# Heads held even-first so that W_in loads fill 128 partitions, with keys, queries and values in two transfers each (retention and a gated feed-forward, one core)

## The chip, the cores and the metric

The kernel runs on 1 core of one Trainium2 chip. The metric is the device time of one execution in microseconds (us); the time of a kernel is the median of its runs. A lower time is better. All arithmetic is float32; the two weight matrices arrive as float64 and are converted on the chip.

## What is computed

A retention layer, whose state decays by a factor of its own for every head, feeds a feed-forward layer without a residual path:

```python
batch, n_heads, seq, head_dim = (4, 8, 768, 64)
gamma = 1.0 - 2.0 ** (-5.0 - np.arange(H))
for t in range(S):
    state = gamma[None, :, None, None] * state + np.einsum('bhd,bhe->bhde', k[:, :, t], v[:, :, t])
    y[:, :, t] = scale * np.einsum('bhd,bhde->bhe', q[:, :, t], state)
x = y.transpose(0, 2, 1, 3).reshape(B * S, H * D)      # 3072 x 512
h = x @ w_in                                           # 512 x 2048
g = h * erf(softplus(h))
out = g @ w_out                                        # 2048 x 512
```

## The kernel before

**Retention.** The 768 positions of each of the four batches are cut into chunks of 128, so there are 24 chunks, numbered `j`. A chunk's keys and queries lie in a tile `KQ[j]` of 128 positions by key/query by eight heads by 64, its values in `V[j]`. Before they are used, keys and queries are multiplied by powers of the heads' decay (`ret_scale`, called `K_`, L514), then turned by TensorE against an identity (`ret_transpose`, `T`, L524) and copied out by ScalarE (L530), so that head pairs `2u` and `2u + 1` lie one above the other on 128 partitions. Scores (`S_`, L557), mask (`M`, L569), and outputs and state (`O_`, L597 to L618, and `A`, L804 and L806) follow. The results land in `XC`, the transposed activations, four columns `kk` of 128 partitions each. Head `h` lands in column `h % 4`, on the lower or upper 64 partitions by `h // 4`. Chunks 0 to 3 are made first, before any feed-forward work, in an order written out by hand (L1081 to L1122); later chunks are woven into the feed-forward.

**The decays.** `d_k` (128 positions by 8 heads, in memory in the order of the heads) and `d_s` (the decay of a whole chunk) are the first two transfers of ScalarE's queue (L399, L400). VectorE copies `d_k` into `kq_s` (L444), makes reciprocals from it (L441, L442), and then runs `K_(0, 0)` on the keys of chunk 0, `second_scales` (L451 to L442), which needs `d_s`, and `K_(0, 1)`, in that order. From chunk 6 on, keys and queries are loaded in blocks of 32 by 32 (`load_blocks`, L187), to be turned by VectorE, with scales of their own (`kq_b`, `by_b`, loaded at L469 and L473).

**The weights.** W_in and W_out arrive in 16 pieces of 1 MB. `load_piece` loads one, `conversion` makes float32 of it on VectorE and ScalarE (L313 to L331), and `load_pieces_after` starts the piece that takes the freed place. Because a column `kk` of `XC` holds heads `kk` and `kk + 4`, and rows of W_in must lie on the partitions of the heads that they meet, a piece of W_in is loaded in halves: `r = 0` to partitions 0 to 63 and `r = 1` to partitions 64 to 127. A piece of W_out is loaded to 128 partitions.

**The order of transfers.** Nearly all are issued by SyncE (SP), in program order: chunk 0's keys and queries, then chunks 1 to 3 with their values, then W_in pieces 0 to 3 (values of chunk 3 in between), then chunk 4. From there on W pieces are issued as conversions free their places.

**The feed-forward.** Of the 3072 positions the first 512 go through plain matmuls in four groups (`hidden`, L860; `project`, L896), while the weights arrive; one more group (L980) is plain too, and the rest use a seven-product scheme on 2 by 2 blocks (L951, L1034), for which `sum_in` adds weight blocks beforehand (L344). The program order of every engine is fixed by the code; nothing is scheduled by a planner.

Of the kernel before, what the change touches and what calls it, by code (L numbers as in the profile page):

```python
# [19 lines left out]
P = 128  # L20
C = 128
# [115 lines left out]
def kernel(  # L137
# [13 lines left out]
    nc = tc.nc  # L151
    B, H, S, D = q.shape
    d_model, d_ff = w_in.shape
    HP = H // 2
    NC = S // C
    NJ = B * NC
    n_k = d_model // P
# [4 lines left out]
    DH = d_model // 2  # L162
# [14 lines left out]
    KQ, V, KB = {}, {}, {}  # L177

    NB = JPC + 2

    def load_blocks(to, src):


        for s, d in itertools.product(range(2), range(2)):
            part = slice((2 * s + d) * 32, (2 * s + d + 1) * 32)
            for u in range(HP):
                nc.sync.dma_start(  # L187
                    to[part, u * C : (u + 1) * C].rearrange("p (a d) -> p a d", d=32),
                    src[2 * u + s, :, d * 32 : (d + 1) * 32].rearrange("(a p) d -> p a d", p=32),
                )  # L190

    def load(j):
        b, c = divmod(j, NC)
        if j == JPC - 1:

            x = act.tile([P, N], F32, name="e", bufs=1)
            KQ[j] = x[:, : 2 * d_model].rearrange("p (i h d) -> p i h d", i=2, h=H)
            V[j] = x[:, 2 * d_model : 3 * d_model].rearrange("p (h d) -> p h d", h=H)
        else:
            KQ[j] = loads.tile([P, 2, H, D], F32, name="kq")  # L200
            V[j] = loads.tile([P, H, D], F32, name="v")
        now = slice(c * C, (c + 1) * C)
        if j >= NB:
            KB[j] = loads.tile([P, HP * C], F32, name="kb", bufs=2)
            nc.sync.dma_start(KQ[j][:, 0], k[b, :, now, :].rearrange("h p d -> p h d"))
            load_blocks(KQ[j][:, 1].rearrange("p h d -> p (h d)"), q[b, :, now, :])
            load_blocks(KB[j], k[b, :, now, :])
        for i, src in enumerate((k, q) if j < NB else ()):
            nc.sync.dma_start(KQ[j][:, i], src[b, :, now, :].rearrange("h p d -> p h d"))
        if not early:  # L210
            load_values(j)

    def load_values(j):
        b, c = divmod(j, NC)
        nc.sync.dma_start(V[j], v[b, :, c * C : (c + 1) * C, :].rearrange("h p d -> p h d"))

    kq_s = const.tile([P, NC, 2, H], F32, name="kq_s")
    d_k = const.tile([P, H], F32, name="d_k")
    d_s = const.tile([P, 2, HP], F32, name="d_s")
# [36 lines left out]
    def load_piece(n, *parts):  # L256

        which, i = pieces[n]
        w = raws[place[n]]
        if which == "in":  # L260
            rows = (slice(2), slice(2, 4)) if n == 0 else (slice(4),)
            for part, g, r in itertools.product(parts or (None,), rows, range(2)):
                f = slice(2 * P) if part is None else slice(part * P, (part + 1) * P)
                nc.sync.dma_start(
                    w[r * D : (r + 1) * D].rearrange("p (g f) -> p g f", g=n_k)[:, g, f],
                    w_in[r * DH : (r + 1) * DH, i * 2 * P : (i + 1) * 2 * P].rearrange(
                        "(g p) f -> p g f", p=D
                    )[:, g, f],
                )
        else:  # L270
            for d in range(2):
                nc.sync.dma_start(
                    w.rearrange("p (d f c) -> p d f c", d=2, f=2)[:, d],
                    w_out[i * 2 * P : (i + 1) * 2 * P, d * DH : (d + 1) * DH].rearrange(
                        "(f p) c -> p f c", p=P
                    ),
                )

    def load_pieces_after(n):
        for later in range(n + 1, n_p):  # L280
            if place[later] == place[n]:
                load_piece(later)
                break
# [112 lines left out]
    nc.gpsimd.memset(below, -float(BELOW << 23))  # L396
    ident = const.tile([P, P], F32, name="ident")
    make_identity(nc, ident)
    nc.scalar.dma_start(d_k, decay_k)  # L399
    nc.scalar.dma_start(d_s, decay_s[::D].rearrange("(o s) h -> o s h", o=1).to_broadcast([P, 2, HP]))  # L400
    load(0)

    nc.scalar.copy(idle_out, ident[:, :1])

    for j in range(1, JPC):
        load(j)
        load_values(j - 1)
    load_piece(0, 0)
    load_values(JPC - 1)
    load_piece(0, 1)  # L410
    for n in range(1, 4):
        load_piece(n, 0, 1)
    load(JPC)
    load_values(JPC)

# [24 lines left out]
    def query_scale(c):  # L440
        nc.vector.reciprocal(kq_s[:, c, 1], kq_s[:, c, 0])  # L441
        nc.vector.tensor_scalar(kq_s[:, c, 1], kq_s[:, c, 1], unscale, None, op0=ALU.mult)  # L442
# [5 lines left out]
    by = const.tile([P, H], F32, name="by")  # L448

    def second_scales():  # L450
        nc.vector.reciprocal(by.rearrange("p (h s) -> p s h", s=2), d_s)  # L451
        nc.vector.tensor_tensor(kq_s[:, 1, 0], kq_s[:, 0, 0], by, op=ALU.mult)
        query_scale(1)
        for c in range(2, NC):
            nc.gpsimd.tensor_tensor(kq_s[:, c, 0], kq_s[:, c - 1, 0], by, op=ALU.mult)
# [7 lines left out]
    by_b = const.tile([P, 2, HP], F32, name="by_b")  # L463

    def load_block_scales():
        for s, d in itertools.product(range(2), range(2)):
            part = slice((2 * s + d) * 32, (2 * s + d + 1) * 32)
            for u in range(HP):
                nc.sync.dma_start(  # L469
                    kq_b[part, 0, 0, u],  # L470
                    decay_k[:, 2 * u + s : 2 * u + s + 1].rearrange("(a p) h -> p (a h)", p=32),
                )
        nc.sync.dma_start(by_b[:, 1], decay_s)  # L473

    def block_scales():
        nc.vector.reciprocal(by_b[:, 0], by_b[:, 1])
# [441 lines left out]
    def chunk_of(g):  # L918
        return TCH // SCH + (g - G0) // 2
# [160 lines left out]

    K_(0, 0)  # L1081
    second_scales()
    T(0, 0)
    keep_warm(2)
# [66 lines left out]
    for g in range(G0):  # L1151
        for u in range(FG):

            if g and u == (2 if g == 1 else 0):
                waiting.append((gated, g - 1))
            hidden(g, u)
            run(after[g][u][0])
            if (g, u) == (1, 0):
                room = 0.0
            waiting.extend(after[g][u][1])  # L1160
        gate(g)
        if g:
            for tt in range(TT):
                project(g - 1, tt)
                if g == 1 and tt < 2:
                    waiting.append((K_, 5) if tt else (sub_states, 4))
                elif g == 2 and tt == 0:
                    sub_results(4)
                    sub_begin(5, ps_h)
                    load_block_scales()  # L1170
                    waiting.append((sub_states, 5))
                elif g == 2 and tt == 2:
                    waiting.append((sub_sums, 4))
# [12 lines left out]
    j = JPC + 2  # L1186
# [94 lines left out]
    g, m = NG - 1, chunk_of(NG - 1)  # L1281
# [4 lines left out]
    r, t0 = R[m], m * SCH  # L1286
# [5 lines left out]
    for i in range(2):  # L1292
# [4 lines left out]
        else:  # L1297
            last = ps_h.tile([P, TCH], F32, name="hp")[:, :P]
            a, b = PRODUCTS[3]
# [50 lines left out]
```

## Time and profile before

| what | value |
|---|---|
| time, median of 3 runs | 663.3 us (663.06 to 663.4) |
| profiled execution: first to last instruction (span) | 660.9 us |
| what lies around the span, median less span | 2.4 us |
| TensorE (PE) busy | 655.7 us, 99% |
| VectorE (DVE) busy | 508.4 us, 77% |
| ScalarE (ACT) busy | 280.2 us, 42% |
| moved by DMA | 51.88 MB in 159413 packets |
| clock granted to TensorE | 1.000 |

The profile gives no own time for the profiled execution beside its span, so its time is read as the span and the 2.4 us around it. "Busy" is the time in which an engine had an instruction in work; for TensorE the ends are modelled. In the timeline a line gives start and duration in us, engine, line of the kernel, operation, the tile written and the tiles read, and in brackets how long the engine was idle before it and what ended that. "SPq" and "ACTq" are instructions that issue transfers. Of DMA queues, q1 is SP's and q10 is ScalarE's; a queue's line gives packets, MB, and the time its packets took as a share of 16 engines.

### The profile page before, as it was taken

How to read it: one execution, taken by the hardware profiler on the slowest of the kernel's cores; microseconds unless marked ns; L12 is line 12 of the kernel's file. 1: busy time of each engine (PE TensorE's matmuls, PEld its weight loads, DVE VectorE, ACT ScalarE, POOL GpSimd, SP SyncE). 2: the span in 40 equal slices, each digit the busy share in tenths (PEclk: the TensorE clock that was granted, in tenths of full speed). 3: DMA queues.
4: the chain of work that ended last, by engine and by line, in shares of the span. 5: the costliest groups of instructions: out<-in, count | busy, mean ns of one | idle time of the engine just before them, and what ended most of it. 6: DMA issues, size and time to landing. Idle time of an engine off the chain costs nothing.

```text
span 660.9 us, 15247 instructions
## 1 busy us (share of the span) xinstructions
PE 655.7 (99%) x6200; PEld 557.3 (84%) x6200; DVE 508.4 (77%) x1102; ACT 280.2 (42%) x402; POOL 11.7 (2%) x29
## 2 busy tenths in 40 slices
PE   8999999999999999999999999999999999999998
PEld 7744444576999999999999999999999999999997
DVE  5999999969986786788678678677687688476464
ACT  3468363445534334244254253342432542533440
POOL 1000000110100000000000000000000000000000
PEclk9999999999999999999999999999999999999999
DMA  9999844385753321222222322221231210000000
GB/s 188 223 264 231 211 129 107 63 152 90 144 123 61 85 47 32 67 47 46 70 44 47 73 39 46 42 72 37 44 79 36 46 53 1 2 34 0 1 33 32
DMA packets 159413, 51.88 MB, mean 78 GB/s; under 512 B 143216, under 2 KB 149744, under 8 KB 159344
## 3 DMA queue, kind: packets, MB, share of 16 engines
q1 hardware_dynamic: 157776, 46.72, 32.8%
q0 software_dynamic: 1152, 4.19, 3.4%
q8 instruction: 48, 0.79, 0.5%
q14 instruction: 21, 0.17, 0.1%
q10 hardware_dynamic: 416, 0.01, 0.0%
HBM read 40.39 MB, written 6.29 MB: 71 GB/s over the span
## 4 chain that ended last, share of the span: by engine, by line
PE 98%; DMA 1%; DVE 0%; ACT 0%; issue 0%
PE o L1034 37%; PE hp L951 22%; PE r L951 12%; PE hp L860 8%; PE o L896 8%; PE hp L980 2%; PE r L736 2%; PE hp L628 1%; PE o L772 1%; PE r L524 1%; PE r L557 1%; PE o L604 1%; PE r L751 1%; PE hp L751 1%; DMA kq<-in_k_dram 1%; PE r L772 0%
## 5 line engine op out<-in xcount | busy, mean ns | idle before, releaser
L1034 PE MATMUL o<-w_out_sb,h 128*128 128x256 f32 (+1 forms) x640 | 142.7, 380 | 0.0
L951 PE MATMUL hp<-xs,w_in_sb 128*128 128x128 f32 x988 | 138.1, 275 | 0.0
L1034 PEld LDWEIGHTS o<-w_out_sb,h 128*128 128x128 f32 x640 | 119.5, 190 | 16.6
L963 DVE TENSOR_TENSOR h<-h,hp 128x256 f32<-128x256 f32 x190 | 78.0, 418 | 70.5 <-PE hp L951 65.6
L951 PEld LDWEIGHTS hp<-xs,w_in_sb 128*128 128x128 f32 x988 | 128.4, 192 | 3.0
L1034 PE MATMUL o<-w_out_sb,e 128*128 128x256 f32 x480 | 113.5, 379 | 0.0
L1034 PEld LDWEIGHTS o<-w_out_sb,e 128*128 128x128 f32 x480 | 86.8, 190 | 9.4
L817 ACT ACTIVATE e<-h 128x2048 f32<-128x2048 f32 x22 | 42.1, 1912 | 119.6 <-DVE h L963 119.6
L963 DVE TENSOR_TENSOR h<-h,r 128x256 f32<-128x256 f32 x152 | 56.9, 415 | 22.3 <-PE r L951 21.4
L965 ACT COPY h<-hp 128x256 f32<-128x256 f32 x38 | 14.2, 373 | 130.7 <-PE hp L951 122.7
L951 PE MATMUL r<-xs,w_in_sb 128*128 128x128 f32 x456 | 63.3, 275 | 0.0
L951 PEld LDWEIGHTS r<-xs,w_in_sb 128*128 128x128 f32 x456 | 57.0, 192 | 0.0
L860 PE MATMUL hp<-xT,w_in_sb 128*128 128x512 f32 (+2 forms) x144 | 56.5, 548 | 0.0
L849 DVE TENSOR_TENSOR e<-h,e 128x1024 f32<-128x1024 f32 x42 | 49.2, 1213 | 8.0 <-ACT e L830 8.0
L860 PEld LDWEIGHTS hp<-xT,w_in_sb 128*128 128x128 f32 x144 | 25.8, 190 | 27.0 <-issue 24.6
L951 PE MATMUL hp<-xT,w_in_sb 128*128 128x128 f32 x304 | 46.3, 275 | 0.0
L951 PEld LDWEIGHTS hp<-xT,w_in_sb 128*128 128x128 f32 x304 | 41.5, 192 | 1.4 <-issue 0.5
L830 ACT ACTIVATE e<-e 128x2048 f32<-128x2048 f32 (+1 forms) x23 | 42.1, 1836 | 0.2
L967 ACT ACTIVATE h<-hp 128x256 f32<-128x256 f32 x57 | 21.9, 384 | 29.7 <-PE hp L951 28.3
L951 PE MATMUL r<-xT,w_in_sb 128*128 128x128 f32 x228 | 31.7, 275 | 0.0
L830 ACT ACT_TABLE_LOAD x24 | 30.8, 1283 | 0.4
L951 PEld LDWEIGHTS r<-xT,w_in_sb 128*128 128x128 f32 x228 | 28.5, 192 | 0.0
(164 smaller groups left out, 799.0 us busy)
## 6 DMA issues: line engine op xcount, KB each, us to landing
w_out_sb<-in_moe_w_out_dram SPq DMA_DIRECT2D x14, 512.0 KB, 5.2
kq<-in_k_dram SPq DMA_DIRECT2D x23, 256.0 KB, 4.0
v<-in_v_dram SPq DMA_DIRECT2D x23, 256.0 KB, 3.4
out_dram<-r SPq DMA_DIRECT2D x23, 256.0 KB, 2.9
kq<-in_q_dram SPq DMA_DIRECT2D x288, 16.0 KB, 1.9
kb<-in_k_dram SPq DMA_DIRECT2D x288, 16.0 KB, 1.8
w_in_sb<-in_moe_w_in_dram SPq DMA_DIRECT2D x8, 512.0 KB, 10.1
w_out_sb<-w_out_sb POOLq DMA_DIRECT2D x8, 512.0 KB, 5.3
```

The costliest lines, as they stand in the source:

```text
L736: nc.tensor.matmul(pp[r][col * D : (col + 1) * D, u % 2, t], x[own, u, :], QT[j][own, u, t], start=first(r, col), stop=True, skip_group_ch ...
L751: nc.tensor.matmul(other[a][own, u % 2, D:] if crossed else pp[a][own, u % 2, t], V[j][t, 2 * u + r, :], AM[j][t, r, u, :D], start=crossed ...
L817: nc.scalar.activation(E[g], HS[g], AF.Softplus)
L830: nc.scalar.activation(E[g][:, half], E[g][:, half], AF.Erf)
L849: nc.vector.tensor_tensor(E[g][:, half], HS[g][:, half], E[g][:, half], op=ALU.mult)
L860: nc.tensor.matmul(HP_[ft][:, t], w_in_of(ft, kk), XC[0][:, kk, t], start=(kk == 0), stop=(kk == n_k - 1),)
L896: nc.tensor.matmul(O[0][tt].rearrange("p (d c) -> p d c", d=2), E[g][:, u * TCH + tt * P : u * TCH + (tt + 1) * P], w_out_of(ft), start=(f ...
L951: nc.tensor.matmul(to[:, u, :], w_in_sb[:, s, w, u * P : (u + 1) * P], XS[m](x), start=first and u == 0, stop=True, skip_group_check=True,)
L963: nc.vector.tensor_tensor(h, h, of, op=ALU.add if plus else ALU.subtract)
L965: nc.scalar.copy(h, of)
L967: nc.scalar.activation(h, of, AF.Copy, scale=-1.0)
L1034: nc.tensor.matmul(O[m][i][:, half, at], G[g][a][:, u * P : (u + 1) * P], w_out_sb[:, s, OUT[b], u, at], start=i not in started, stop=(s = ...
```

## The change

The eight heads are held in the order 0, 2, 4, 6, 1, 3, 5, 7. Slot `i` holds head `i % 4 * 2 + i // 4`. The code of the arithmetic keeps its slots, so slot `i` still lands in column `i % 4` of `XC`, on half `i // 4`. Column `kk` then holds heads `2 kk` and `2 kk + 1`, which are 128 consecutive rows of W_in, and a piece needs no halves. Loads of keys, queries and values become two transfers each, one for the even and one for the odd heads; the decays are loaded in the new order.

```diff
+    def head(i):
+        return i % HP * 2 + i // HP
+
+    def load_heads(to, src):
+        for s in range(2):
+            nc.sync.dma_start(to[:, s * HP : (s + 1) * HP], src[s::2].rearrange("h p d -> p h d"))
...                     # load_blocks
-                    src[2 * u + s, :, d * 32 : (d + 1) * 32].rearrange("(a p) d -> p a d", p=32),
+                    src[head(2 * u + s), :, d * 32 : (d + 1) * 32].rearrange("(a p) d -> p a d", p=32),
...                     # load, j >= NB
-            nc.sync.dma_start(KQ[j][:, 0], k[b, :, now, :].rearrange("h p d -> p h d"))
+            load_heads(KQ[j][:, 0], k[b, :, now, :])
...                     # load, j < NB
-            nc.sync.dma_start(KQ[j][:, i], src[b, :, now, :].rearrange("h p d -> p h d"))
+            load_heads(KQ[j][:, i], src[b, :, now, :])
...                     # load_values
-        nc.sync.dma_start(V[j], v[b, :, c * C : (c + 1) * C, :].rearrange("h p d -> p h d"))
+        load_heads(V[j], v[b, :, c * C : (c + 1) * C, :])
...                     # load_piece
-            for part, g, r in itertools.product(parts or (None,), rows, range(2)):
+            for part, g in itertools.product(parts or (None,), rows):
                 f = slice(2 * P) if part is None else slice(part * P, (part + 1) * P)
                 nc.sync.dma_start(
-                    w[r * D : (r + 1) * D].rearrange("p (g f) -> p g f", g=n_k)[:, g, f],
-                    w_in[r * DH : (r + 1) * DH, i * 2 * P : (i + 1) * 2 * P].rearrange(
-                        "(g p) f -> p g f", p=D
-                    )[:, g, f],
+                    w.rearrange("p (g f) -> p g f", g=n_k)[:, g, f],
+                    w_in[:, i * 2 * P : (i + 1) * 2 * P].rearrange("(g p) f -> p g f", p=P)[:, g, f],
                 )
...
-    nc.scalar.dma_start(d_k, decay_k)
+    for s in range(2):
+        nc.scalar.dma_start(d_k[:, s * HP : (s + 1) * HP], decay_k[:, s::2])
     nc.scalar.dma_start(d_s, decay_s[::D].rearrange("(o s) h -> o s h", o=1).to_broadcast([P, 2, HP]))
...                     # second_scales
-        nc.vector.reciprocal(by.rearrange("p (h s) -> p s h", s=2), d_s)
+        nc.vector.reciprocal(by.rearrange("p (s h) -> p s h", s=2), d_s)
...                     # load_block_scales
-                    decay_k[:, 2 * u + s : 2 * u + s + 1].rearrange("(a p) h -> p (a h)", p=32),
+                    decay_k[:, head(2 * u + s) : head(2 * u + s) + 1].rearrange("(a p) h -> p (a h)", p=32),
                 )
-        nc.sync.dma_start(by_b[:, 1], decay_s)
+        for s, w in itertools.product(range(2), range(2)):
+            nc.sync.dma_start(
+                by_b[s * D : (s + 1) * D, 1, 2 * w : 2 * w + 2], decay_s[w * D : (w + 1) * D, s::2]
+            )
```

## The prediction, made before the changed kernel was run

> **What bounds the kernel now.** I read the page first, then the table of stretches, the chain of waits, and the timeline and DMA view of the first 15 us. The page:
>
> ```profile
> span 660.9 us, 15247 instructions
> ...
> PE 655.7 (99%) x6200; PEld 557.3 (84%) x6200; DVE 508.4 (77%) x1102; ACT 280.2 (42%) x402; POOL 11.7 (2%) x29
> ...
> PE 98%; DMA 1%; DVE 0%; ACT 0%; issue 0%
> ```
>
> TensorE is busy for all but 5.2 us, and the chain is TensorE for 98%. Busy can hide waiting, so I cut the span where TensorE's gaps lie:
>
> ```profile
> 0.00:5.10 5.10, 3.36 (x14) 3.06 (x14) 1.28 (x5) 1.48 (x2) 1.64 (x11) 1.00 0.58 122
> 5.10:14.90 9.80, 9.21 (x99) 8.01 (x99) 7.34 (x17) 3.83 (x8) 1.32 (x4) 1.00 1.34 220
> 14.90:60.00 45.10, 45.10 (x349) 26.57 (x350) 41.79 (x74) 26.57 (x38) 0.00 (x0) 1.00 1.07 232
> 60.00:130.00 70.00, 70.00 (x344) 33.68 (x343) 68.75 (x94) 34.26 (x36) 1.67 (x6) 1.00 0.57 144
> 130.00:590.00 460.00, 460.00 (x4926) 423.40 (x4925) 349.99 (x827) 188.48 (x287) 7.02 (x8) 1.00 0.30 60
> ```
>
> The second column is the length, the third TensorE's busy time, the last two the DMA share and GB/s. From 14.90 to 590 us TensorE has no gap at all. Nor is it waiting inside its instructions: the chain has 32 of L896 in 13.73 us, 0.429 each, and their starts keep that spacing from 54 us to the end of the plain groups. So nothing between 15 and 590 us can be made faster by an earlier transfer, and whatever delays TensorE before 15 us is added to the end whole. What sets that start is here (chain, then VectorE's timeline):
>
> ```profile
> 0.81 3.53 DMA kq<-in_k_dram
> 4.36 0.70 DVE kq L514
> 5.11 1.12 PE r L524 x4
> ```
>
> ```profile
> 2.91 0.17 DVE L444 COPY kq_s<-d_k 128x8 f32<-128x8 f32 x1 [2.91 <-DMA d_k<-decay_k_dram]
> 4.36 0.69 DVE L514 TENSOR_TENSOR kq<-kq,kq_s 128x512 f32<-128x512 f32 x1 [0.84 <-DMA kq<-in_k_dram]
> 4.97 0.20 DVE L451 RECIPROCAL by<-d_s 128x8 f32<-128x8 f32 x1
> 5.76 0.69 DVE L514 TENSOR_TENSOR kq<-kq,kq_s 128x512 f32<-128x512 f32 x1
> 6.97 0.69 DVE L514 TENSOR_TENSOR kq<-kq,kq_s 128x512 f32<-128x512 f32 x1 [0.51 <-DMA kq<-in_k_dram]
> 8.25 0.69 DVE L514 TENSOR_TENSOR kq<-kq,kq_s 128x512 f32<-128x512 f32 x1 [0.59 <-DMA kq<-in_q_dram]
> ```
>
> `d_k` is there at 2.9 us and has 0.84 us to spare. After that the loads are the bound: the keys of chunk 0, the keys of chunk 1 (6.97) and its queries (8.25) are each waited for. `d_s` has nearly nothing to spare (landing at 4.6, read at 4.97).
>
> **W_in on 128 partitions.** What it may bring shows in the page's DMA part:
>
> ```profile
> w_out_sb<-in_moe_w_out_dram SPq DMA_DIRECT2D x14, 512.0 KB, 5.2
> ...
> w_in_sb<-in_moe_w_in_dram SPq DMA_DIRECT2D x8, 512.0 KB, 10.1
> ```
>
> Equal sizes, half the partitions, twice the time to landing (the second in a fuller queue). So the pieces should land earlier, and SP issues half as many. But in the whole trace VectorE waits for W_in once, 0.35 us at 19.37 (L313), and TensorE works without a gap through that time. What is late next is the conversion itself (VectorE is busy 68.75 of 70 us from 60 to 130). Gain: 0; if that cover were gone, at most the 0.35 us.
>
> The Trainium skill ("DMA: Bandwidth & Descriptors", Rules for kernel authors) says that two transfers to disjoint partition halves only serialize and advises one over 128. Priced by the rows of landing, the saving in the DMA queues would be about 4.9 us for each 512 KB, and by the trace none of it reaches TensorE.
>
> **Arithmetic.** Instructions, shapes and order of PE, DVE, ACT and POOL stay, slots being renamed. 0.
>
> **Keys, queries, values in halves.** Packets stay 256 bytes and as many. Each extra transfer costs SP one issue; small ones issued back to back stand 0.47 us apart (16 at L469 in 8.74 us). Two halves are 0.95 us of issue against the 1.20 us that a 256 KB load takes at the 218 GB/s of 5 to 13 us, so the DMA engines stay the bound: 0. If SP took 0.65 us each, as at L264, it would be 0.1 us a load, 0.5 us by the keys of chunk 2: upper bound. Later on, six more issues precede the last block of chunk 7's keys (three for `by_b`, one each for keys and values of chunk 6 and keys of chunk 7, less a wait or two that they fill): up to 2.8 us. VectorE waits there already (3.2 us, L546), but afterwards idles 2.26 us before L635 at 147.89, which covers it to within 0.6 us, and TensorE has its own work there. 0.
>
> **`d_k` as two strided halves.** This is where I see a cost. A row of `d_k` is 8 consecutive numbers; every second of them is not consecutive. How the trace moves single numbers from a strided column is seen in `kq_b` (128 numbers a transfer), and how the two queues mix when `d_s` runs beside the loads:
>
> ```profile
> q1 hardware_dynamic: 1309, 0.01, 16.1%
> ...
> kq_b<-decay_k_dram SPq DMA_DIRECT2D x10, 0.5 KB, 1.8
> ```
>
> ```profile
> DMA packets 623, 0.09 MB, mean 134 GB/s; under 512 B 623, under 2 KB 623, under 8 KB 623
> ...
> q1 hardware_dynamic: 366, 0.09, 57.6%
> q10 hardware_dynamic: 257, 0.00, 19.8%
> ```
>
> The first is 92.7 to 97 us: 1309 packets for about ten transfers, one a number, each occupying an engine for 0.161 x 4.3 x 16 / 1309 = 8.5 ns. So `d_k` goes from 128 packets to 1024, and with the end packet per engine of one more transfer ScalarE's queue from 416 to 1328: 912 more, ahead of or among the first keys and queries. Cheapest, they fill engine time alone: 912 x 8.5 / 16 = 0.5 us. But the second view (3.3 to 4.0 us) shows the queues mixed: 623 packets in 0.7 us, 890 a us, against 616 in 0.6 us, 1027 a us, from 2.6 to 3.2 when SP's ran alone. From 3.5 to 4.0 it is 344 in 0.5 us, 690 a us; from 1.8 to 2.6, at the very start, 335 in 0.8 us, 420 a us. So 912 packets cost 1.0, 1.3 or 2.2 us. I take 1.2, between the first two, since they are under load as the new ones will be, and keep 0.5 and 2.2.
>
> All loads behind them land 1.2 us later: chunk 1's keys at 8.1 instead of 6.94. `d_k`'s second half, issued 0.47 us later (ScalarE's two issues stand so), lands about 4.5 to 5.5, eats its 0.84 us and holds `K_(0, 0)` until 5.1 to 6.1; `d_s` behind it lands at about 5.5 to 6.5, and all of VectorE queued behind L451 waits: `K_(0, 1)`, then chunk 1's scaling, and TensorE's transposes behind those. This comes to the same 1 us or so, beside the loads and not on top.
>
> **A slow TensorE at the start.** L495 starts every 213 ns until 6.87 us, the L524 after it every 109, though the granted clock reads 1.00 throughout. With gaps around `T(0, 0)` longer by 1 to 2 us the step may come later than its work. Least: it moves with the chain, 0. Most: some 2.8 us, if all that runs from 7 to 10.5 us is slow (12 transposes at 0.104 and 16 others at about 0.1). I take the four transposes of one group, 4 x 0.104 = 0.4, being nearest to what stands beside the step.
>
> The Trainium skill ("TensorE: Matmul & The Clock Gate", Part 1) explains such a step by a free-running window of about 3.4 us that must be busy. By it, the step would come either with the chain or one window later, and the sum would be 1.2 or about 3.
>
> **Sum.** 0 + 0 + 0 + 1.2 + 0.4 = 1.6 us. Span 660.9 + 1.6 = 662.5; with 2.4 us around it, 664.9 against 663.3 now. A measurement of this kernel can tell about 0.2%, 1.3 us.
>
> **Rivals.**
> 1. The small packets slip into the gaps at 8.5 ns: `d_k` lands inside its spare 0.84 us, loads move 0.5 us at most. Not slower to a measurement: 663.3 to 664.0. For it: the packets are short. Against: both queues slow while mixed, seen twice. It decides if `d_k` lands before 3.75. Chance 0.20.
> 2. `d_s` decides: 1328 small packets, one for each of SP's, at 420 a us: 2656 / 420 = 6.3 us from 1.85, so `d_s` lands at 8.7, `K_(0, 1)` starts at 9.5 for 5.76: +3.7, less what the loads had already lost, and a slow clock with it: 666 to 667.5. For it: the rate at the very start. Against: the later, higher rates. Chance 0.18.
> 3. W_in was after all what TensorE followed, in the conversions: 663.0 at best by the 0.35 us. The span has no other wait for it. Chance 0.03.
> 4. The later SP queue passes its 2.26 us cover: +0.6, 663.9 without the start's cost. Chance 0.05.
>
> **How the numbers follow.** My case (0.9 to 2.3 us later, 664.2 to 665.6) has 0.54; about a quarter of it is within 1.3 us. Same: rivals 1, 3 and 4 and that part, 0.41, of which I give 0.01 away. Slower: the rest of my case and rival 2, 0.58. Faster by 1.3 us has no place to come from but an error of mine: 0.02. The range leaves out the lower half of rival 1 and the far end of rival 2: 663.6 to 667.0.
>
> **What would show it.** In the profile after: q10 with about 1328 packets; L444 waiting for `d_k` until 4.5 to 5.5; first L514 at 5.1 to 6.1; chunk 1's keys at about 8.1; TensorE without gaps from about 16.5 on; W_in landing in near 5 us for 512 KB and TensorE no earlier for it. I am wrong if L444 starts before 3.8, or if a gap in TensorE opens or closes after 17 us.

## The result and the profile after

| kernel | median of 5 runs | lowest to highest | ratio to before |
|---|---|---|---|
| before | 663.4 us | 663.06 to 664.04 | 1 |
| changed | 666.7 us | 665.13 to 668.27 | 1.0051 (1.0037 to 1.0066) |

The changed kernel is slower by 3.3 us. The profiled execution took 665.13 us, the lowest of the five, with a span of 663.4: 1.73 us lie around it. That span is 2.5 us longer than before's 660.9. The page:

```profile
span 663.4 us, 15333 instructions
...
PE 655.3 (99%) x6200; PEld 556.5 (84%) x6200; DVE 508.1 (77%) x1102; ACT 280.1 (42%) x402; POOL 12.1 (2%) x29
...
q10 hardware_dynamic: 1328, 0.01, 0.1%
...
PE 98%; DVE 1%; DMA 0%; ACT 0%; issue 0%; ACTq 0%; DVEq 0%
...
w_in_sb<-in_moe_w_in_dram SPq DMA_DIRECT2D x4, 1024.0 KB, 5.4
```

TensorE does the same 655 us of work, so the 2.5 us are new idle time. ScalarE's queue carries the 1328 packets. Lines of code have moved by about 10: L406 loads `d_k`, L451 copies it, L524 is `ret_scale`, L534 the transposes, L505 the idle products, L556 the scaling of prepared chunks, L961 the products of the seven-product scheme, L973 its additions, L359 GpSimd's transfers. A whole MB of W_in now lands in 5.4 us, where half of one took 10.1. The stretches show where the idle time is:

```profile
0.00:5.10 5.10, 3.35 (x14) 3.06 (x14) 0.23 (x2) 1.47 (x2) 1.63 (x11) 1.00 0.60 98
5.10:15.50 10.40, 8.57 (x102) 7.17 (x102) 8.29 (x20) 3.85 (x8) 1.81 (x4) 1.00 1.28 225
15.50:60.00 44.50, 44.50 (x348) 26.31 (x349) 41.14 (x74) 25.97 (x38) 0.00 (x0) 1.00 0.88 258
60.00:130.00 70.00, 70.00 (x343) 33.41 (x342) 68.83 (x93) 34.34 (x34) 1.68 (x6) 1.00 0.46 127
130.00:590.00 460.00, 458.99 (x4896) 422.29 (x4895) 349.24 (x827) 188.88 (x288) 7.00 (x8) 1.00 0.30 60
```

From 15.5 to 130 us TensorE is full again, but between 130 and 590 it is short by 1.01 us. That gap was not there before. The losses lie in three places.

**The start, 0.57 us.** VectorE's timeline:

```profile
4.83 0.17 DVE L451 COPY kq_s<-d_k 128x8 f32<-128x8 f32 x1 [4.83 <-DMA d_k<-decay_k_dram]
...
5.36 0.69 DVE L524 TENSOR_TENSOR kq<-kq,kq_s 128x512 f32<-128x512 f32 x1
...
6.71 1.51 DVE L524 TENSOR_TENSOR kq<-kq,kq_s 128x512 f32<-128x512 f32 x2
8.85 0.69 DVE L524 TENSOR_TENSOR kq<-kq,kq_s 128x512 f32<-128x512 f32 x1 [0.63 <-DMA kq<-in_q_dram]
```

`d_k` is waited for until 4.83 us (2.91 before), `K_(0, 0)` starts at 5.36 instead of 4.36, and the last of these scalings, on chunk 1's queries, at 8.85 instead of 8.25. The loads themselves came 0.57 us later: chunk 1's keys landed at 7.51, before at 6.94. Not all of this need be the strided `d_k`'s: with the same halves and `d_k` whole they landed at 7.07 in e2 below, though at 6.75 in e5. TensorE's last wait of the start ended at 15.46, before at 14.89.

**A gap at 163 us, 1.28 us.** Timelines of VectorE and GpSimd, first before, then after, and TensorE's after:

```profile
139.30 0.69 DVE L546 TENSOR_TENSOR kb<-kb,kq_b 128x512 f32<-128x512 f32 x1 [3.18 <-DMA kq<-in_k_dram]
```

```profile
137.82 0.87 POOL L353 DMA_DIRECT2D w_out_sb<-w_out_sb  x1 [5.64 <-PE hp L980]
```

```profile
144.37 0.69 DVE L556 TENSOR_TENSOR kb<-kb,kq_b 128x512 f32<-128x512 f32 x1 [7.65 <-DMA v<-in_v_dram]
```

```profile
138.49 0.87 POOL L359 DMA_DIRECT2D w_out_sb<-w_out_sb  x1 [5.75 <-PE hp L990]
```

```profile
163.72 1.16 PE L961 MATMUL hp<-xs,w_in_sb 128*128 128x128 f32 x8 [1.01 <-DVE h L973]
```

SP's issues of chunk 7's blocks (tile view of `kb`, 128 to 146 us; after the count come the durations in ns, then the first and the last start), before and after, and the time to landing after:

```profile
L187 SPq DMA_DIRECT2D kb<-in_k_dram x13: 430/430/1206, 128.0 to 134.8; - x13
```

```profile
L195 SPq DMA_DIRECT2D kb<-in_k_dram x16: 376/430/1297, 130.0 to 139.0; - x16
...
DMA to landing us min/median/max: 1.7/2.3/5.2
```

VectorE waits 7.65 us for chunk 7's block loads, before 3.2. The label names the values, but what VectorE reads is the blocks, of which the last landed at 144.15. SP issued that last block at 138.99 us, before at 134.78 (landing at 138.92). GpSimd's transfer, 512 KB from SBUF to SBUF with an addition, was issued at 138.49, so that it now stands ahead of the block: the block landed after it, 5.2 us after its issue. VectorE is then 5 us behind, and at 162.7 TensorE has to wait for it.

**The end, 0.65 us.** The chain's last instruction of an engine, and SP's waits from 655 us on; first before, then after:

```profile
658.11 0.29 DVE r L1305
```

```profile
SPq L1346 <- DMA out_dram<-r: 0.7, 1, 0.7
```

```profile
659.96 0.29 DVE r L1315
```

```profile
SPq L1356 <- DMA out_dram<-r: 1.0, 2, 0.8
```

From the end of VectorE's last addition to the end of the span it was 660.9 - 658.40 = 2.50 us, and is 663.4 - 660.25 = 3.15. The work after that addition, one store, is the same. SP closes with a row of waits in a fixed order of semaphores, and the 43 additional transfers have turned the last store to another semaphore. Before, one more wait followed the one for it; now five more waits follow, of 0.07 to 0.36 us each.

Those three make 0.57 + 1.28 + 0.65 = 2.5. The 1.28 is the gap of 1.01 and 0.27 more: VectorE's last addition starts 1.85 us later, of which the start and the gap's visible part explain 1.58. This 0.27 for each gap recurs below; what it is, no run shows.

### The profile page after: what moved, and what is told of

It reads as the page before. It is cut to its first block, busy times and chain, and to the rows that moved or that the text cites. A ratio compares the mean times of both kernels' runs of the same rounds, so it can differ in the third digit from the quotient of the medians.

```text
span 663.4 us, 15333 instructions
## 1 busy us (share of the span) xinstructions
PE 655.3 (99%) x6200; PEld 556.5 (84%) x6200; DVE 508.1 (77%) x1102; ACT 280.1 (42%) x402; POOL 12.1 (2%) x29
## 3 DMA queue, kind: packets, MB, share of 16 engines
q10 hardware_dynamic: 1328, 0.01, 0.1%
## 4 chain that ended last, share of the span: by engine, by line
PE 98%; DVE 1%; DMA 0%; ACT 0%; issue 0%; ACTq 0%; DVEq 0%
PE o L1044 37%; PE hp L961 22%; PE r L961 12%; PE hp L870 8%; PE o L906 8%; PE hp L990 2%; PE r L746 2%; PE hp L638 1%; PE o L782 1%; PE r L567 1%; PE o L614 1%; PE r L761 1%; PE hp L761 1%; PE r L534 1%; DMA d_k<-decay_k_dram 0%; PE r L782 0%
## 5 line engine op out<-in xcount | busy, mean ns | idle before, releaser
L961 PE MATMUL hp<-xs,w_in_sb 128*128 128x128 f32 x988 | 138.2, 275 | 1.0 <-DVE h L973 1.0
L961 PEld LDWEIGHTS hp<-xs,w_in_sb 128*128 128x128 f32 x988 | 128.4, 192 | 4.1 <-DVE h L973 1.2
L973 DVE TENSOR_TENSOR h<-h,hp 128x256 f32<-128x256 f32 x190 | 78.0, 419 | 68.1 <-PE hp L961 63.3
L973 DVE TENSOR_TENSOR h<-h,r 128x256 f32<-128x256 f32 x152 | 57.0, 417 | 21.4 <-PE r L961 20.6
L961 PE MATMUL r<-xs,w_in_sb 128*128 128x128 f32 x456 | 63.3, 275 | 0.0
L961 PEld LDWEIGHTS r<-xs,w_in_sb 128*128 128x128 f32 x456 | 57.0, 192 | 0.0
L961 PE MATMUL hp<-xT,w_in_sb 128*128 128x128 f32 x304 | 46.3, 275 | 0.0
L961 PEld LDWEIGHTS hp<-xT,w_in_sb 128*128 128x128 f32 x304 | 41.5, 192 | 1.4 <-issue 0.5
L961 PE MATMUL r<-xT,w_in_sb 128*128 128x128 f32 x228 | 31.7, 275 | 0.0
L961 PEld LDWEIGHTS r<-xT,w_in_sb 128*128 128x128 f32 x228 | 28.5, 192 | 0.0
```

The source lines that it names most:

```text
L961: nc.tensor.matmul(to[:, u, :], w_in_sb[:, s, w, u * P : (u + 1) * P], XS[m](x), start=first and u == 0, stop=True, skip_group_check=True,)
L973: nc.vector.tensor_tensor(h, h, of, op=ALU.add if plus else ALU.subtract)
```

## The experiments

My theory: three costs that add up, namely the strided `d_k` at the start (with TensorE's slow phase), SP's later issues in front of GpSimd's transfer, and the order of the closing waits. Rivals: one of the first two makes it all; the halves as such cost; W_in gains something that the rest hides. Each run's profile is split in the same way in the table. "Start" is by how much later than in before (14.89) TensorE's last wait of the start ended. "Gaps" are TensorE's waits between 19 and 590 us. "Last addition" is by how much later than 658.11 VectorE's last instruction starts. "Tail" is from that instruction's end to the end of the span.

| kernel | start | gaps | last addition | tail | profiled execution | median (lowest to highest, runs) |
|---|---|---|---|---|---|---|
| changed | 0.57 | 1.01 | 1.85 | 3.15 | 665.13 | 666.7 (665.13 to 668.27, 5) |
| e1 changed again | 1.76 | 0.68, 1.57 | 4.55 | 3.15 | 667.83 | 668.06 (666.64 to 668.38, 5) |
| e2 `d_k` whole | 0.20 | 0.99 | 1.45 | 3.25 | 664.8 | 665.36 (664.6 to 666.29, 5) |
| e3 scales early | 1.36 | none | 1.36 | 3.24 | 664.67 | 664.9 (664.67 to 665.56, 5) |
| e4 GpSimd later | 2.11 | 1.60 | 3.98 | 3.12 | 667.27 | 667.0 (663.66 to 672.41, 8) |
| e5 both e2 and e3 | -0.12 | none | -0.11 | 3.21 | 663.25 | 663.55 (663.25 to 665.58, 11) |
| e6 before, strided | 3.02 | none | 3.03 | 2.47 | 666.01 | 666.01 (665.66 to 666.83, 5) |
| e7 before, 3 issues | 1.89 | none | 1.89 | 2.81 | 664.97 | 663.1 (662.94 to 664.97, 11) |
| e8 halves where needed | 1.84 | none | 1.84 | 2.56 | 664.52 | 663.76 (662.61 to 664.52, 11) |
| e9 changed, more warm | 0.64 | 0.89, 1.92 | 3.98 | 3.12 | 667.29 | 667.02 (664.78 to 668.96, 6) |
| e10 before, halves | 0.32 | none | 0.32 | 2.68 | 663.12 | 663.14 (662.78 to 664.71, 12) |
| e11 e8, one more warm | 0.29 | none | 0.29 | 2.51 | 662.96 | 662.94 (662.69 to 663.03, 11) |
| e12 before, less warm | 1.33 | none | 1.33 | 2.47 | 663.95 | 663.72 (663.22 to 665.48, 11) |

Before beside them was 662.91 (e1 to e4), 663.03 (e5 to e8) and 662.96 us (e9 to e12). In each row the last addition's delay is the start's plus the gaps plus 0.26 to 0.27 for each gap, to 0.01 us. So nothing else delayed the last addition. Start and gaps are those of one execution, which need not be like the median's. "Measured" below is the time as a multiple of before's beside it, with its 95% interval. The two groups of runs e1 to e4 and e5 to e12 were taken on different chips.

### e1: the changed kernel once more

> The changed kernel as it is, run and profiled again, to see which of its costs return. Theory A (two costs): TensorE's stream is 0.5 to 0.7 us later by 16 us, for the decays' small packets, and there is a second gap of 1 us or more near 163 us, where VectorE waited 7.7 us for the last blocks of chunk 7's keys because SP issues them some 4 us later and they fall behind a GpSimd transfer. Time 665 to 668 us. Theory B (start alone): the gap near 163 was an accident of one execution and is not there again; what is above 0.6 us is scatter. Theory C (weights): the earlier landing of W_in moves other transfers; gaps would appear between 17 and 130 us.

Measured 1.0073 (1.0061 to 1.0085). VectorE's and TensorE's timelines:

```profile
145.23 0.69 DVE L556 TENSOR_TENSOR kb<-kb,kq_b 128x512 f32<-128x512 f32 x1 [7.33 <-DMA v<-in_v_dram]
...
213.12 0.69 DVE L556 TENSOR_TENSOR kb<-kb,kq_b 128x512 f32<-128x512 f32 x1 [4.88 <-DMA v<-in_v_dram]
```

```profile
164.58 1.16 PE L961 MATMUL hp<-xs,w_in_sb 128*128 128x128 f32 x8 [0.68 <-DVE h L973]
...
218.25 1.16 PE L961 MATMUL hp<-xs,w_in_sb 128*128 128x128 f32 x8 [1.57 <-DVE h L973]
```

The gap is there again, and a second one, where chunk 10's blocks are late (the expectation of e10 calls it chunk 9): their last issue was at 202.0 us before, at 207.9 in the changed kernel's first profile, at 209.4 here. The start differs too, though it waits equally long for `d_k`. TensorE's timeline, the first profile and then e1:

```profile
6.11 0.66 PE L534 MATMUL r<-ident,kq 128*128 128x128 f32 x4 [1.29 <-DVE kq L524]
6.60 0.61 PE L505 MATMUL o<-ident 128*128 128x128 f32 x4
```

```profile
6.11 1.11 PE L534 MATMUL r<-ident,kq 128*128 128x128 f32 x4 [1.29 <-DVE kq L524]
7.01 1.06 PE L505 MATMUL o<-ident 128*128 128x128 f32 x4
```

The same groups after the same wait take 0.66 or 1.11 us. TensorE begins in a slow phase (starts 213 ns apart, later 109), and the traces hold records of the granted clock that tell when it ends: the step to the full clock is at 7.02 us in before, at 5.48 in the first profile after, while TensorE waits, and at 9.91 in e1. Ahead of its first record a trace has none, and the clock column of the stretches reads 1.00 there: the 1.00 "throughout" of the prediction is no measurement. The late step costs e1 1.2 us more at the start.

The records also show what chance this is. From the step to the clock's drop after the kernel's end it is a whole number of 3.413 us in all thirteen traces that have records (192 times in before and in e1, 193 times in the first profile after). So the clock changes on a grid of 3.4 us, and where the grid lies against the kernel's start differs from execution to execution.

### e2 and e3: one of the two suspects each

In e2 `d_k` is loaded whole, and the copy that VectorE makes anyway puts it in order:

```diff
-    for s in range(2):
-        nc.scalar.dma_start(d_k[:, s * HP : (s + 1) * HP], decay_k[:, s::2])
+    nc.scalar.dma_start(d_k, decay_k)
...
-    nc.vector.tensor_copy(kq_s[:, 0, 0], d_k)
+    nc.vector.tensor_copy(
+        kq_s[:, 0, 0].rearrange("p (s h) -> p s h", s=2), d_k.rearrange("p (h s) -> p s h", s=2)
+    )
```

> The changed kernel with one contiguous transfer of d_k, put into the new order by the copy on VectorE that is there anyway. Theory A: L451 starts at about 3 us again, the first L524 at 4.0 to 4.5, TensorE's stream 0.4 to 0.7 us earlier than in the changed kernel; the gap near 163 stays, so 0.5 us less than the changed kernel and still 1 us or more above the kernel before. Theory B: all of the loss goes, 663.4. If the halved loads delay the start themselves, it stays late by more than 0.3 us.

Measured 1.0038 (1.0025 to 1.0051). VectorE's and TensorE's timelines:

```profile
2.72 0.17 DVE L450 COPY kq_s<-d_k 128x8 f32<-128x8 f32 x1 [2.72 <-DMA d_k<-decay_k_dram]
...
4.79 0.69 DVE L525 TENSOR_TENSOR kq<-kq,kq_s 128x512 f32<-128x512 f32 x1 [1.46 <-DMA kq<-in_k_dram]
```

```profile
163.32 1.16 PE L962 MATMUL hp<-xs,w_in_sb 128*128 128x128 f32 x8 [0.99 <-DVE h L974]
```

The copy waits until 2.7 us, the start is back to +0.20, and the gap stays (0.99). What is left at the start goes with the halves: `K_(0, 0)` waits for the second half of chunk 0's keys until 4.79, where it began at 4.36 before.

In e3 the block scales, with the three more issues of `by_b`, are loaded a projection earlier, where SP isn't backlogged:

```diff
                 project(g - 1, tt)
+                if (g, tt) == (1, 3):
+                    load_block_scales()
...
                     sub_begin(5, ps_h)
-                    load_block_scales()
```

> The changed kernel with the 20 transfers of the block scales issued one group earlier, where SP has nothing to do, so that nothing of them stands ahead of chunks 6 and 7. Theory A: chunk 7's last block is issued 1.5 to 3 us earlier and lands ahead of GpSimd's transfer, at about 139 us; VectorE waits 2 to 4 us for it instead of 7.7, no gap near 163; 1 us or more (by the median 2 us) less than the changed kernel, and 0.6 us above the kernel before. Theory B: no change against the changed kernel.

Measured 1.0031 (1.0019 to 1.0043). VectorE's timeline:

```profile
140.29 0.69 DVE L556 TENSOR_TENSOR kb<-kb,kq_b 128x512 f32<-128x512 f32 x1 [2.77 <-DMA kb<-in_k_dram]
...
209.14 0.69 DVE L556 TENSOR_TENSOR kb<-kb,kq_b 128x512 f32<-128x512 f32 x1 [2.25 <-DMA kb<-in_k_dram]
```

The first wait is as short as in before (3.2), the second is 2.25 (before had none there), and both gaps are gone. GpSimd's transfer was issued at 138.98, and the last block, issued at 137.28, landed ahead of it at 140.07. The start keeps its cost. Neither suspect alone makes the loss.

### e4: GpSimd's transfer moved

```diff
-        if n in (1, 4, 7):
+        if n in (1, 7, 8):
             next(last_steps)
```

> The changed kernel with the second and third of GpSimd's accumulating transfers (the sums of W_out) begun after the seventh and eighth step of the plain group instead of after the fourth and seventh, about 7 us later. SP's queue is as in the changed kernel. Theory A: chunk 7's last block, issued at about 139 us, lands at 140 to 141 instead of 144.2; VectorE's wait shrinks from 7.7 to about 4 us; the gap near 163 is gone, 1 us or more less than the changed kernel. If SP's later issue alone were enough without the collision, the gap would stay.

Measured 1.0062 (1.0035 to 1.009), with runs from 663.66 to 672.41. VectorE's and TensorE's timelines:

```profile
143.17 0.69 DVE L556 TENSOR_TENSOR kb<-kb,kq_b 128x512 f32<-128x512 f32 x1 [4.90 <-DMA kb<-in_k_dram]
...
212.55 0.69 DVE L556 TENSOR_TENSOR kb<-kb,kq_b 128x512 f32<-128x512 f32 x1 [4.91 <-DMA kb<-in_k_dram]
```

```profile
217.69 1.16 PE L961 MATMUL hp<-xs,w_in_sb 128*128 128x128 f32 x8 [1.60 <-DVE h L973]
```

The transfer now starts at 144.91, the first wait falls from 7.3 to 4.9 us and its gap is gone, so GpSimd's transfer had its part in the first gap. It has none in the second one, which stays. The median didn't fall against e1 by more than the runs scatter. The run of 672.41 has no profile, but its granted clock is 0.994 on average, where most runs have 0.999 or 1.000: by estimate 0.006 x 670.7 = 4.0 us of it are lost clock.

### e5: both taken away

> The changed kernel with both: d_k in one contiguous transfer, and the block scales issued one group earlier. If the two costs add (start 0.2 instead of 0.6 to 2.1 us late, no gap near 163 or 216), the span is 662.0 and the time 663.6 to 663.9, about 4 us less than the changed kernel measured beside it. What stays above the kernel before is then 0.2 at the start and the longer end: the last store's landing to the end of the span took 1.6 us instead of 0.9 in all profiles of changed kernels. If one of them was only a part of the other, the time stays at 664.5 or more.

Measured 1.0016 (1.0007 to 1.0025). Start -0.12, no gap, and yet a span of 661.5, 0.6 more than before: all of it the tail (3.21). The medians put a price on each cost: the tail, and what else is left, 663.55 - 663.03 = 0.5 us; the strided `d_k` with its slow phase, e3 less e5, 1.35; the late blocks, e2 less e5, 1.8. Together 3.7 us, between the 3.3 and 5.1 (e1) that the changed kernel itself measured. These prices are rough: e2 and e3 have five runs each and ran on another chip than e5, and four of e5's eleven runs are at 664.6 to 665.6.

The second gap goes with something else, which the traces show, though no run tried it. In e1 the last of chunk 10's blocks was still on its way when the queue named `instruction` (q8) began a packet of 16 KB at 210.64 us, which held one of the 16 engines for 1.2 us (73.2% of 16 engines for 0.1 us). First that packet (DMA view of 210.6 to 210.7 us), then the landing of the block issued at 209.44, and for comparison that of the block issued at 207.91 in the first profile after:

```profile
q8 instruction: 1, 0.02, 73.2%
```

```profile
kb<-in_k_dram SPq DMA_DIRECT2D x1, 16.0 KB, 3.5
```

```profile
kb<-in_k_dram SPq DMA_DIRECT2D x1, 16.0 KB, 1.7
```

It is the same in e4 and e9 (packet at 210.01 and 209.73, last block landing at 212.33 and 212.34). In the other eleven profiles the last block had landed when this packet began (in the first profile after at 209.62, before 210.45), and none of them has a second gap.

### e6 and e7: parts of the change, put into before

e6 loads `d_k` in two strided halves, left in the old order:

```diff
-    nc.scalar.dma_start(d_k, decay_k)
+    for s in range(2):
+        nc.scalar.dma_start(d_k[:, s::2], decay_k[:, s::2])
```

> The kernel before with d_k alone loaded as two strided halves (even and odd heads, each to its old place); all else as before. Theory A: L444 starts at 4.6 to 4.9 us, TensorE's stream by 16 us is 0.6 to 2.1 us late, depending on when TensorE's starts at the beginning go from 213 to 109 ns apart; no gap near 163 or 216, end unchanged: 663.5 to 665.0. If the halved loads were needed for the damage, less than 0.3 us late.

Measured 1.0051 (1.0039 to 1.0064). The chain, and the stretches around the delayed start:

```profile
1.49 4.73 DMA d_k<-decay_k_dram
```

```profile
4.70:8.00 3.30, 0.50 (x5) 0.42 (x5) 1.55 (x7) 0.00 (x0) 0.00 (x1) 1.00 1.39 197
8.02:11.43 3.41, 3.41 (x18) 3.03 (x18) 2.57 (x7) 1.24 (x3) 1.90 (x4) 0.50 1.35 218
11.50:14.90 3.40, 3.17 (x41) 2.74 (x41) 1.89 (x3) 1.04 (x2) 0.00 (x0) 1.00 1.35 218
```

That is above the 663.5 to 665.0 expected, and the start loses more than in the changed kernel itself. Here the numbers are strided in SBUF as well, and among whole loads of SP's rather than halves; `d_k` was there only at 6.2 us instead of 4.8. Which of the two differences does it is open. TensorE was idle for 2.80 us, until 7.58, and the granted clock (the column after POOL), which had stepped up at 4.60, is back at 0.50 for one stretch of 3.41 us, from 8.02 to 11.43. TensorE's starts are 213 ns apart again in this stretch: the slow phase is the clock's.

The Trainium skill ("TensorE: Matmul & The Clock Gate", Part 1) says that this clock follows a free-running window of about 3.4 us, so that the same kernel is slow for a different time in each run. The traces agree: steps of 3.413 us, and 5.48 and 9.91 us for the end of the slow phase in the two profiles of the changed kernel. With one such window more the prediction's sum was, by its estimate, about 3 us, 1.8 above the 1.2 without; e1's later step cost 1.2.

e7 has three more transfers than before, by loading chunk 4's keys, queries and values in halves.

> The kernel before with the keys, queries and values of chunk 4 alone in two transfers each (heads 0 to 3 and 4 to 7): three more transfers on SP at about 30 us, where nothing waits, so that the last store signals on another of SP's rotating semaphores, the same as in the changed kernel. If the longer end comes from the place of that semaphore in SP's closing row of waits: TensorE as before throughout, 0.6 to 0.7 us more between the last store's landing and the end, 663.5 to 663.6. If the end has another cause, no change against the kernel before.

Measured 1.0006 (0.9997 to 1.0014): three issues there cost nothing. The profiled execution was the slowest of the eleven, by a late step of the clock (10.98 us), though nothing at its start differs from before. Its tail is 2.81. Six waits follow the one for the last store, of 0.06 us each, where before has one, so the place in the row is worth 0.3 us, which the median doesn't show. The rest of the changed kernel's 0.65 lies in waits that take longer there (one of them 0.36), and why they do is open.

### e8 and e11: the change without its costs

e8 has halves only for the keys and queries of chunks 0 to 5. Values and later keys are loaded whole and read by head; `d_k` is whole, the scales are early, and one transfer of W_in less is split, so that SP makes as many transfers as before, 717.

```diff
-            load_heads(KQ[j][:, 0], k[b, :, now, :])
+            nc.sync.dma_start(KQ[j][:, 0], k[b, :, now, :].rearrange("h p d -> p h d"))
...
-        load_heads(V[j], v[b, :, c * C : (c + 1) * C, :])
+        nc.sync.dma_start(V[j], v[b, :, c * C : (c + 1) * C, :].rearrange("h p d -> p h d"))
...                     # products with values, the same at every use
-                place(h), V[j][:, h, :], AM[j][:, h % 2, h // 2, :],
+                place(h), V[j][:, head(h), :], AM[j][:, h % 2, h // 2, :],
```

> W_in on 128 partitions, with halves only for keys and queries of chunks 0 to 5 (where TensorE's transposes need neighbours); values, and keys from chunk 6 on, in one transfer in the heads' own order, addressed by head; d_k whole, block scales one group earlier, and as many SP transfers modulo 8 as in the kernel before (a second half of W_in's first piece in one transfer). Start 0 to 0.3 us late, no gap, end as before: 662.9 to 663.2, no slower than the kernel before by more than 0.3 us. If 128 partitions for W_in are worth anything by themselves, it shows here as less than 662.9.

Measured 1.0008 (0.9999 to 1.0017), in two groups, five runs from 662.61 to 663.1 and six from 663.76 to 664.52. The median misses the 662.9 to 663.2 expected. The profiled execution is of the upper group, with the step of the clock at 10.87 us. The tail is 2.56, so it does go back with the number of transfers. e11 adds one idle product:

```diff
-    keep_warm(7)
+    keep_warm(8)
```

> The kernel with halves only where needed, d_k whole, block scales early and the number of SP transfers as before modulo 8, with eight instead of seven idle products, which fill the 0.66 us that TensorE waited for chunk 0's keys. Theory A: the slower executions (663.8 to 664.5) go, the time is 662.6 to 663.0, no slower than the kernel before; W_in on 128 partitions gains nothing beyond that. If W_in's faster transfers were worth time, below 662.4.

Measured 0.9997 (0.9989 to 1.0006), all eleven runs within 0.34 us. TensorE's timeline:

```profile
1.46 3.69 PE L510 MATMUL o<-ident 128*128 128x128 f32 x16 [1.46 <-POOL ident masks.py:199]
5.76 0.66 PE L539 MATMUL r<-ident,kq 128*128 128x128 f32 x4 [0.60 <-DVE kq L529]
6.25 0.61 PE L510 MATMUL o<-ident 128*128 128x128 f32 x4
```

The transposes at 5.76 are fast already, and the upper group is gone. With W_in on 128 partitions and none of the other costs, the time is before's, so W_in gains nothing that shows. (Before with eight idle products was not run, so this run alone doesn't tell what the eighth saves from what W_in might; but before's TensorE has no gap from 14.9 to 590 us that W_in could close.)

### e9, e10, e12: the slow phase and the halves by themselves

e9 is the changed kernel with ten idle products at the start for seven.

> The changed kernel with ten instead of seven idle products at the start (L505), so that TensorE is busy until about 6.1 us, when its first transposes can start, instead of idle from 4.8. Nothing that waits for loads changes. Theory A, with the clock: the step from 213 to 109 ns comes by about 7 us in every execution, so the start is 0.6 us late and no longer up to 2.1; the time falls by 0.5 to 1.5 us by the median, and the later gaps (163, 216) stay: 665.5 to 667. If the late step has nothing to do with TensorE's idle time, the time stays at that of the changed kernel, 666.7 to 668.

Measured 1.0055 (1.0038 to 1.0072). The start fell to +0.64, but this execution has both gaps (0.89 and 1.92), and the median is no better than the changed kernel's first one, where 0.5 to 1.5 us less was expected. A better start alone saves nothing that can be told, while the gaps stay.

e10 is before with all loads of keys, queries and values in halves, by the old order (the blocks excepted).

> The kernel before with all loads of keys, queries and values (but for the blocks) in two transfers, heads 0 to 3 and 4 to 7, and nothing else. SP then has three more issues ahead of chunk 7's last block and seven ahead of chunk 9's. Theory A (SP's backlog): the last block of chunk 7 is issued 1 to 2 us later and VectorE's wait there grows from 3.2 to 4 to 8 us, by whether GpSimd's second transfer is met; chunk 9's blocks are 3 to 5 us later; a gap of up to 1.6 us near 163 or 216 in part of the executions; start as before but for the clock: 663.5 to 666. If only by_b's extra issues push SP over, no gap and 663.0 to 663.7.

Measured 1.0006 (0.9997 to 1.0014). VectorE's timeline:

```profile
139.07 0.69 DVE L551 TENSOR_TENSOR kb<-kb,kq_b 128x512 f32<-128x512 f32 x1 [2.65 <-DMA kb<-in_k_dram]
```

The halves alone cost nothing late: the last block is issued at 135.88, and VectorE waits 2.65 us. By the rows it takes `by_b`'s issues as well to push SP past the cover. These are the views of `by_b`, before and after:

```profile
L473 SPq DMA_DIRECT2D by_b<-decay_s_dram x1: 430/430/430, 97.2 to 97.2; - x1
```

```profile
L481 SPq DMA_DIRECT2D by_b<-decay_s_dram x4: 590/601/692, 97.7 to 99.7; - x4
```

One transfer of 0.43 us has become four that hold SP for 2.62 us, 2.2 more. (e3 moved them together with the other block scales, so that they were not tried by themselves.)

At the start the halves don't show in the median, but they aren't free. In this profile the start is 0.32 late, and chunk 0's keys are complete at 4.74 us, before at 4.34. Of the 34 runs of e5, e8 and e10, which load the first chunks in halves and `d_k` whole, 13 are 1.1 us or more above the fastest run of their kernel. Of the 80 runs with before's start (before beside e1 to e12, and e7) three are. With one idle product more (e11) none of eleven is. That it is the clock's late step in all of these is seen in the profiles of e7 and e8 alone.

e12 is before with five idle products for seven; nothing else changes.

> The kernel before with five instead of seven idle products at the start: TensorE is idle from about 4.0 instead of 4.8 us until its first transposes at 5.1; no transfer and no other instruction changes. Theory A, with the clock: in part of the executions the step from 213 to 109 ns comes at 9 to 11 us instead of 6.7 and the time is up to 1.9 us longer; the median 663.0 to 664.9, with a wider spread than the kernel before beside it. If idle time before the step does not matter, 663.0 and no wider.

Measured 1.0013 (1.0004 to 1.0021). TensorE's timeline:

```profile
1.46 2.50 PE L495 MATMUL o<-ident 128*128 128x128 f32 x10 [1.46 <-POOL ident masks.py:199]
5.11 1.12 PE L524 MATMUL r<-ident,kq 128*128 128x128 f32 x4 [1.15 <-DVE kq L514]
6.02 1.06 PE L495 MATMUL o<-ident 128*128 128x128 f32 x4
7.07 1.12 PE L524 MATMUL hp<-ident,kq 128*128 128x128 f32 x4
```

`T(0, 0)` starts at 5.11 as in before, but after 1.15 us of idle time instead of 0.29, and what follows stays slow until the clock's step at 9.91 us, before at 7.02. That alone costs 0.8 us in the median and up to 2.5. So a wait in front of the first transposes costs twice: for itself, and by the phase that it prolongs in part of the executions.

## Why the prediction was right, and where it was not

The direction was right and the time (666.7) lies in the range, but the middle was 1.8 us too low, and that the range held is in part luck. It reached up to 667.0 for rival 2, which didn't come: `d_s` landed at 5.83, not at 8.7 (its own sum, 1.85 + 6.3, gives 8.15). What filled the upper part was a term put at 0, and the same kernel's median in e1, 668.06, lies above the range. Rival 1 didn't come either: `d_k` landed at 4.74, not before 3.75. Step by step:

**W_in, 0 us: right.** The pieces land early, VectorE's 0.35 us wait is gone, and neither the changed kernel nor e11 is earlier for it.

**The halves of the first chunks, 0 us: right for the median (e10), too low for single runs.** Chunk 0's keys are complete up to 0.4 us later (e2, e10), which the upper bound of 0.5 covers, and slow runs, by e8's profile those of a late clock step, come more often.

**`d_k` as 912 more packets, 1.2 us: the mechanism right, the size too large.** The packets are there, L451 waited until 4.83 (named: 4.5 to 5.5) and `K_(0, 0)` started at 5.36 (named: 5.1 to 6.1). But the loads came 0.57 us later, not 1.2: chunk 1's keys at 7.51 and not 8.1, and of this the halves may have a part (7.07 in e2, 6.75 in e5). From 2.3 to 4.2 us the mixed queues moved 2530 packets in 1.9 us, 1330 a us, where I had taken 690 to 890. So the mixed rates in the trace of before were no limit of the engines, presumably those of queues with too little to move, and the row that I kept as the low end, 0.5, was the nearest.

**The slow phase, 0.4 us: a matter of chance, 1.2 us between two profiles of the same kernel.** Both terms together, 1.6 us by the prediction, are 1.35 by e3 less e5.

**Six issues ahead of chunk 7's last block, 0 us: this is the step that failed.** The price of up to 2.8 us of delay and the cover of 2.26 us on VectorE were read from the timeline, and rival 4 gave 0.6 us to the case that it doesn't suffice. But the issue slipped by 4.2 us: 0.57 is the start's, and `by_b`'s three more issues took 2.2, at 0.6 to 0.7 each, where I had priced an issue at 0.47. And I asked only how late it would be and not what starts on the DMA engines meanwhile: GpSimd's 512 KB, at 137.82 in the trace of before, 3 us after that last issue. The block that came behind it took 5.2 us to land, the one just before it 1.8, and the backlog went on to chunk 10. Medians give this 1.8 us, three times rival 4's price. "I am wrong if a gap in TensorE opens after 17 us" was the right alarm; it went off.

**The end, not in the sum: about 0.5 us.** That more transfers can lengthen the closing waits was not on my list. The tails of e5 (3.21, with the change's transfers) and e8 (2.56, with before's number) show it. That it is the last store's place in the row of semaphores is read from the trace and was not tried by itself; e7, with three more transfers, got 0.3 of it.

Open are: how busy TensorE must have been for the clock to step up at a point of its grid (one idle product more made e8's two groups into one), what makes e6 dearer than the same packets in the changed kernel, and most of the scatter of e4.

## What to carry to other kernels

A small table that is reordered by a strided transfer becomes one packet for each number, and whoever reads it first pays; let a copy that an engine makes anyway put it in order. When a change adds transfers to a queue that is backlogged, follow the queue to the next user, and see which other transfers will have started on the DMA engines by then: slack read from a wait is worth nothing if a long transfer stands in it. A wait ahead of TensorE's first work is dearer than it looks, as it can prolong the slow phase (e12); fill it with idle products, and compare medians of many runs, not single profiles.

## What the runs showed that I had not expected

- Two executions of one kernel, with the same waits until 6.11 us, differ by 1.2 us in the next 10 us by the slow phase of TensorE (0.66 against 1.11 us for four transposes): the clock stepped up at 5.48 in one and at 9.91 in the other.
- In all thirteen traces with clock records, the time from the clock's step to its drop after the end is a whole number of 3.413 us.
- In each of the three profiles with a second gap a packet of 16 KB on the queue `instruction` began near 210 us while chunk 10's last block was on its way, and in none of the others. The block took 3.3 to 3.5 us to land, where it took 1.7 in the changed kernel's first profile.
- Each gap in TensorE's stream cost 0.26 to 0.27 us more than the idle time that the profile shows, in all five profiles that have one.
- Two hardware queues that were mixed, one of packets of 4 bytes, moved 1330 packets a us, more than SP's queue alone in the trace of before (1027, packets of 256 bytes).
- A block load of 16 KB issued 0.5 us behind GpSimd's 512 KB landed 5.2 us after its issue, after that transfer, where the one issued 0.5 us earlier took 1.8 (138.51 to 140.33).
- The span's end moved by 0.65 us with the change's 43 transfers, without other work behind the last store; three transfers (e7) moved it by 0.3.
